# Block-sparse attention with a channel mix: wide units for the two end blocks only, scores in row groups by key slot, 32x32 turns on VectorE

## The chip, the cores and the metric

One core of one Trainium2 chip. The metric is the device time of one execution in microseconds; the median of three runs of the kernel before is 604.21 us (603.62 to 605.64).

## The reference

Two stages follow each other. The first is attention over 4 batches, 8 heads, 768 positions of 64 numbers, in blocks of 32 positions (24 blocks). A query block sees block 0, block 23, itself, its two neighbours and three blocks drawn at random; query blocks 0 and 23 see all. The second is a channel mix over the 512 joined channels.

```python
scores = scale * np.matmul(q, k.transpose(0, 1, 3, 2))
mask = np.abs(blk_i - blk_j) <= window                      # window = 1
mask = mask | (blk_i == 0) | (blk_j == 0) | (blk_i == n_blocks - 1) | (blk_j == n_blocks - 1)
for qb in range(n_blocks):
    for kb in sampled_blocks[qb]:                           # three, drawn; can repeat or be seen already
        mask[qb * block:(qb + 1) * block, kb * block:(kb + 1) * block] = True
scores = np.where(mask, scores, -1000000000.0)
attn = softmax(scores)                                      # rows' maximum subtracted, sum + 1e-09
x = attn @ v                                                # to (4, 768, 512)

xk = mu_k * x + (1.0 - mu_k) * x_prev                       # x_prev: x one position earlier
xr = mu_r * x + (1.0 - mu_r) * x_prev
k = np.maximum(xk @ w_k, 0.0)                               # 512 -> 1024
v = k * k @ w_v                                             # 1024 -> 512
r = 1.0 / (1.0 + np.exp(-(xr @ w_r)))
out = r * v
```

The three weights come as 64-bit floats and are narrowed on the chip.

## The kernel before

**Units.** Attention is cut into 24 units. Per batch there is one wide unit (u = 0) with the four query blocks 21, 22, 23 and 0 on 128 partitions, which takes scores against all 768 keys, and five near units (u = 1 to 5) with four consecutive query blocks each, 1 to 20. A query block of a near unit has eight slots of 32 keys: its neighbourhood (3), blocks 0 and 23, the three drawn. `load_unit` (L415) brings them by DMAs from SP's queue into one of five tiles KR per query block (the drawn ones at addresses read from `packed`), and the values into one of six tiles VR: the neighbourhood by a DMA on SP, block 23 and the drawn ones by an indirect gather on GpSimd (L470).

**A near unit** works in two groups (`near_group`), each of four heads. Scores `s` (L524): for each pair of heads, query block and head a product of 64 x 32 weights (the queries) with 256 key columns; two row halves and four column strips of the array work side by side. `soft` (L479, VectorE) scales, adds a mask per slot (a slot drawn twice, or seen already, gets a large number) and takes the row minimum in one pass, 256 columns at a time; `exp` (L489, ScalarE) follows with a sum of each row; `turn` (L500) turns 128 x 128 pieces on TensorE (PE) into `t`, copied to `pt` by VectorE (L506); the values `o` (L546) are products with 128 x 32 weights from `pt` and 64 columns of VR. `finish` divides by the sums, turns x (L606) and copies it into `xt`.

**A wide unit** (`wide_pair`) does the same for each pair of heads with 768 keys: `sw` (L563), `tw` (L500), `o` (L585).

**The mixer** handles each of 12 tiles of 256 positions: `split_x` forms xr and xk and splits them into two parts of lower precision, `gate` (L713, r), `hidden` (L731, h, then relu, square and its split), `values` (L760, v) with three products per term, and a last multiplication on VectorE (L768) and store (L771). `weight` narrows the weights at the start.

**Order.** Every operation is handed to `Plan.add` with its engine, a duration in ns, a rank, and what it reads and writes. `Plan.order` places all of them by these durations and ranks, and each engine's program is written out in that order; nothing is decided on the chip. The constants at the end of the file (O_MAX, LEAD_K and so on) set ranks and the earliest time that a load is placed. In the order before, the wide units of batches 0, 1 and 2 come first, those of batches 2 and 3 are kept in DRAM (`away`) and read back; the mixer's tiles have ranks at equal distances.

Sixteen KB of PSUM per partition are shared by s (two tiles of two banks), t (2), o (1) and m (1, the mixer's products).

Of the kernel before, what the change touches and what calls it, by code (L numbers as in the profile page):

```python
# [8 lines left out]
F32 = mybir.dt.float32  # L9
F32R = mybir.dt.float32r  # L10
I32 = mybir.dt.int32
# [5 lines left out]
DRAM = bass.MemoryType.DRAM  # L17

P = 128
# [10 lines left out]
QB, NC, SLOTS = 4, 5, 8  # L30

WIDE_BLOCKS = (NB - 3, NB - 2, NB - 1, 0)
SEEN = 5
FAR = 8e9

# [43 lines left out]
class Op:  # L79
    __slots__ = ("engine", "ns", "lag", "fn", "rank", "deps", "users", "bufs", "end", "start", "table", "seq", "waits", "release", "size")  # L80


class Plan:
# [13 lines left out]
    def add(self, engine, ns, rank, fn, reads=(), writes=(), lag=0, table=None, release=0.0, size=0):  # L97
# [5 lines left out]
        op.bufs, op.release, op.size = [], release * 1000, size  # L103
# [29 lines left out]

    def order(self):
        free, table, avail = {}, {}, {}
        queue_free = 0.0
# [6 lines left out]
        while len(placed) < len(self.ops):  # L143
            best = None
            for engine, ops in avail.items():
                now = free.get(engine, 0.0)
                cand = []
                for op in ops:
                    at = max(now, op.release)
                    for d in op.deps:  # L150
                        at = max(at, d.end + (self.HOP[d.engine] if d.engine != engine else self.SAME.get(engine, 60)) + d.lag)
# [7 lines left out]
                    if at is not None:  # L159
                        cand.append((at, op))  # L160
                if cand:
                    first = min(c[0] for c in cand)
                    now_on = table.get(engine)
                    at, op = min((c for c in cand if c[0] <= first + NEAR),
                                 key=lambda c: (c[1].rank - STAY * (c[1].table is not None and c[1].table == now_on), c[1].seq))
                    if best is None or at < best[0]:
                        best = (at, op)
            assert best is not None, "no operation can start"
            at, op = best
# [6 lines left out]
            op.start, op.end = at, at + ns  # L176
            free[op.engine] = op.end
            if op.size:
                ready = op.end + (self.RING_POOL if op.engine == "POOL" else self.RING)
                queue_free = max(queue_free, ready) + op.size / self.RATE  # L180
                op.lag = queue_free + self.DONE - op.end
            for buf in op.bufs:
# [22 lines left out]
AWAY = 2  # L205


def unit_time(i):

    wides = sum(u == 0 for b, u in UNITS[:i])  # L210
    others = min(i, len(UNITS)) - wides
    return A_FIRST + A_WIDE * wides + A_SOON * min(others, SOON) + A_STEP * max(others - SOON, 0)
# [3 lines left out]
def block_sparse_attention_channel_mix(  # L216
    ctx: ExitStack, tc: tile.TileContext,
    kt, kd, kq, qt, vt, vw, blocks, rows, picks, consts, mu_k, mu_r, w_k, w_v, w_r, out, wide,
# [5 lines left out]
    dr = ctx.enter_context(tc.tile_pool(name="scratch", bufs=1, space=DRAM))  # L224
# [14 lines left out]
    k_ring = buf([P, K_RING, S], F32, "k2", 1, "k_ring")  # L239
# [3 lines left out]
    number = fixed([1, NB * NRAND * 2], I32, "number")  # L243

    packed = fixed([1, NB], I32, "packed")
    lines = fixed([P, B, NC * QB], I32, "lines")
    near_mask = fixed([P, NC, SLOTS], F32, "near_mask")
    wide_mask = fixed([P, NB], F32, "wide_mask")
    mk = fixed([P, 2, CC], F32, "mk")
    early_w = buf([P, EARLY_W, 512, 2], I32, "wv", 1, "early_w")  # L250
    away = [Fixed(dr.tile([P, CC, P], F32, name=f"away{b}")) for b in range(B - AWAY)]


    def mask_setup():
        own = buf([P, NC + 1, NRAND, 2], I32, "kk", 3, "own")
        con = buf([P, NC * (SEEN + SLOTS) + 2 * NB + 2], F32, "zr", 3, "con")
        pick = buf([P, NC * QB, 2], I32, "kk", 3, "pick")
        f = buf([P, NC + 1, NRAND], F32, "dif", 2, "ownf")
        same = buf([P, NB * NRAND], F32, "x0", 1, "same")
        word = buf([P, 2 * NB], F32, "x1", 1, "word")  # L260
        line = buf([P, NC * QB], F32, "pt", PT_BUFS, "line")
        near = NC * SEEN
        stat = near + NC * SLOTS
        plan.add(SP, ISSUE, -30, lambda: nc.sync.dma_start(number.ap, blocks), writes=[(number,)], size=2000)
        plan.add(ACT, ISSUE, -32, lambda: nc.scalar.dma_start(own.ap.rearrange("p a b c -> p (a b c)"), rows), writes=[(own,)], size=20000)
        plan.add(ACT, ISSUE, -31, lambda: nc.scalar.dma_start(con.ap, consts), writes=[(con,)], size=60000)
        plan.add(ACT, ISSUE, PICK, lambda: nc.scalar.dma_start(pick.ap.rearrange("p a b -> p (a b)"), picks), writes=[(pick,)], size=20000)
# [11 lines left out]

        def find():  # L280
            v = nc.gpsimd
            c = con.ap
            v.tensor_copy(out=line.ap, in_=pick.ap[:, :, 0])
            v.tensor_scalar(out=line.ap, in0=line.ap, scalar1=c[:, stat + 2 * NB : stat + 2 * NB + 1],
                            scalar2=c[:, stat + 2 * NB + 1 : stat + 2 * NB + 2], op0=ALU.mult, op1=ALU.add)
            for b in range(B):
                v.tensor_scalar(out=lines.ap[:, b, :], in0=line.ap, scalar1=float(b * S), scalar2=None, op0=ALU.add)

        plan.add(DVE, 600, -15, pack, reads=[(number,)], writes=[(word,), (packed,)])
        plan.add(POOL, 900, PICK + 3, find, reads=[(con,), (pick,)], writes=[(line,), (lines,)])  # L290

        def far():
            v = nc.vector
            v.tensor_copy(out=f.ap, in_=own.ap[:, :, :, 0])
            c = con.ap

            e = same.ap.rearrange("p (a b) -> p a b", b=NRAND)
            v.tensor_tensor(
# [614 lines left out]
```

## Time and profile before

| | |
|---|---|
| median of three runs | 604.21 us |
| span of the profiled execution (its own time is not given beside it) | 616.1 us |
| TensorE busy (matmul) | 575.8 us, 93% |
| TensorE weight loads | 465.5 us, 76% |
| VectorE, ScalarE, GpSimd busy | 303.8, 300.6, 344.0 us |
| matmuls; instructions in all | 8172; 20666 |
| bytes moved by DMA | 114.18 MB, mean 185 GB/s |
| PE's share of the chain that ended last | 63% |

The span runs from the first to the last instruction. Rows of the profile give line, engine, operation, the names of what is written and read, shapes and count, then busy time and the mean of one, then the engine's idle time just before and what ended it; "issue" there is idle time that ended for nothing the profile shows. Rows of the timeline give start and length. Rows of stretches give for each engine busy time and count, then the granted clock of TensorE, the mean busy share of the 16 DMA engines, and GB/s.

### The profile page before, as it was taken

Reading aid. Unit: us, or ns where it says so; the run is one execution under the profiler, and the core shown is the slowest. Engines: PE = TensorE matmul, PEld = TensorE weight load, DVE = VectorE, ACT = ScalarE, POOL = GpSimd, SP = SyncE. Lnnn points to the kernel's source line nnn. Section 1 sums busy time; section 2 is a strip of 40 time slices with the busy share of each in tenths; the row PEclk is TensorE's granted clock in tenths of the full one; section 3 lists DMA queues with packets and bytes.
Section 4 is the critical chain, followed back from the end, with each engine's and each line's share of the span. In section 5 each row is a group of like instructions: output and inputs, shape, how many; then the busy total and the mean of one; then the engine's idle time right before and its main releaser. Section 6 shows DMA issues by size and latency. Waiting matters only on the chain.

```text
span 616.1 us, 20666 instructions
## 1 busy us (share of the span) xinstructions
PE 575.8 (93%) x8172; PEld 465.5 (76%) x8172; DVE 303.8 (49%) x906; ACT 300.6 (49%) x712; POOL 344.0 (56%) x400
## 2 busy tenths in 40 slices
PE   8887878798899999999999989999999999999997
PEld 3564655587667878878788778778778788989897
DVE  6677768873864255264443452653632532423300
ACT  3675845583544545355535534635545454333341
POOL 1324344865777737657836835546467464664551
PEclk9999989999899999999999999999999999999999
DMA  8959659858786667766764774774666620000001
GB/s 310 399 157 379 231 168 335 282 164 286 219 261 217 188 193 212 210 181 202 227 200 164 232 227 146 233 229 147 224 188 182 201 75 1 36 18 18 17 18 35
DMA packets 88499, 114.18 MB, mean 185 GB/s; under 512 B 12626, under 2 KB 59219, under 8 KB 88403
## 3 DMA queue, kind: packets, MB, share of 16 engines
q1 hardware_dynamic: 81570, 91.79, 46.7%
q0 software_dynamic: 6400, 20.98, 10.7%
q8 instruction: 65, 1.06, 0.7%
q10 hardware_dynamic: 432, 0.10, 0.2%
q14 instruction: 32, 0.25, 0.1%
HBM read 106.01 MB, written 6.82 MB: 183 GB/s over the span
## 4 chain that ended last, share of the span: by engine, by line
PE 63%; DVE 10%; ACT 8%; issue 6%; POOL 5%; DMA 3%; another core or an unknown queue 2%; SPq 2%; ACTq 0%; DVEq 0%; POOLq 0%
PE v L760 17%; PE o L546 5%; PE h_1p L731 5%; PE h_3p L731 5%; PE r_0p L713 5%; PE t L500 5%; PE r_1p L713 4%; PE h_2p L731 4%; ACT p L489 4%; PE s L524 3%; PE h_0p L731 2%; PE tw L500 2%; PE sw L563 2%; PE o L585 2%
## 5 line engine op out<-in xcount | busy, mean ns | idle before, releaser
L760 PE MATMUL v<-wv,k 128*128 128x512 f32 (+1 forms) x600 | 139.4, 386 | 1.4 <-DVE z L768 1.4
L760 PEld LDWEIGHTS v<-wv,k 128*128 128x128 f32 x600 | 107.5, 188 | 26.5 <-DVE xr_2f L680 2.1
L489 ACT ACTIVATE p<-p,nm 128x256 f32<-128x256 f32 x160 | 79.4, 498 | 48.7 <-DVE nm L479 48.7
L470 POOL DMA_INDIRECT VR<-vt,lines x80 | 79.0, 988 | 33.1 <-PE o L546 16.0
L506 DVE COPY pt<-t 128x512 f32<-128x512 f32 x80 | 53.0, 686 | 81.5 <-PE t L500 74.6
L479 DVE CUSTOM_DVE_ANT_1 p<-s,near_mask 128x256 f32<-128x256 f32 x160 | 57.9, 418 | 30.4 <-remote 19.4
L689 POOL TENSOR_TENSOR xr<-xr_1f,xr 128x256 fp32r<-128x256 f32 x24 | 17.7, 740 | 72.0 <-ACT xr L687 71.9
L524 PE MATMUL s<-KR,q 64*32 64x256 f32 x1280 | 50.8, 381 | 1.0 <-PE tw L500 0.9
L500 PE MATMUL t<-ident,p 128*128 128x128 f32 x320 | 47.5, 283 | 3.8 <-ACT p L489 2.3
L546 PEld LDWEIGHTS o<-VR,pt 128*32 128x32 f32 x2560 | 37.9, 110 | 15.0 <-issue 8.8
L546 PE MATMUL o<-VR,pt 128*32 128x64 f32 x2560 | 44.7, 221 | 2.3 <-issue 1.4
L687 ACT CAST xr<-xr_1f 128x256 fp32r<-128x256 f32 x24 | 9.7, 405 | 72.9 <-PE r_0p L713 43.0
L731 PE MATMUL h_1p<-xk,wk 128*128 128x256 f32 x288 | 37.0, 283 | 8.2 <-ACT h_0k L744 4.6
L609 DVE TENSOR_TENSOR x<-o,R 128x512 f32<-128x512 f32 x24 | 16.6, 691 | 56.8 <-PE o L546 53.7
L500 PEld LDWEIGHTS t<-ident,p 128*128 128x128 f32 x320 | 36.9, 144 | 9.3 <-ACT p L489 6.4
L731 PEld LDWEIGHTS h_1p<-xk,wk 128*128 128x128 f32 x288 | 34.7, 188 | 10.3 <-ACT h_0k L744 5.5
L731 PEld LDWEIGHTS h_0p<-xk,wk 128*128 128x128 f32 x288 | 34.9, 188 | 3.6 <-issue 3.3
L713 PE MATMUL r_1p<-wr,xr 128*128 128x512 f32 x144 | 37.7, 411 | 0.0
L524 PEld LDWEIGHTS s<-KR,q 64*32 64x32 f32 x1280 | 27.1, 105 | 13.8 <-issue 3.8
L731 PE MATMUL h_3p<-xk,wk 128*128 128x256 f32 x288 | 36.8, 282 | 0.4 <-ACT h_2k L744 0.4
L731 PEld LDWEIGHTS h_2p<-xk,wk 128*128 128x128 f32 x288 | 34.6, 188 | 3.3 <-ACT k L745 3.3
L731 PE MATMUL h_0p<-xk,wk 128*128 128x256 f32 x288 | 36.9, 283 | 0.0
(115 smaller groups left out, 1043.7 us busy)
## 6 DMA issues: line engine op xcount, KB each, us to landing
VR<-vw SPq DMA_DIRECT2D x80, 256.0 KB
KR<-kd SPq DMA_DIRECT2D x80, 192.0 KB
KR<-kt SPq DMA_DIRECT2D x240, 64.0 KB
k_ring<-kq SPq DMA_DIRECT2D x16, 384.0 KB
VR<-vt SPq DMA_DIRECT2D x24, 256.0 KB
q<-qt SPq DMA_DIRECT2D x23, 256.0 KB
out<-z SPq DMA_DIRECT2D x23, 256.0 KB
early_w<-w_k SPq DMA_DIRECT2D x8, 512.0 KB
```

The lines of the kernel that those rows point to most:

```text
L470: plan.add(POOL, GATHER, at - LEAD_V + 0.01 * j, lambda w=w, n=n: nc.gpsimd.indirect_dma_start(VR[w].ap[:, 1, :], None, vt.rearrange("b n ...
L479: nc.vector.tensor_tensor_reduce(out=p.ap[:, cs].rearrange("p (a x) -> p a x", x=BLK), in0=view().rearrange("p (a x) -> p a x", x=BLK), in ...
L489: plan.add(ACT, 280 + 0.83 * (cs.stop - cs.start), rank, lambda: nc.scalar.activation(p.ap[:, cs], p.ap[:, cs], AF.Exp, bias=nm.ap[:, col ...
L500: nc.tensor.transpose(tp.ap[:, i, :], p.ap[:, cs], ident.ap)
L506: plan.add(DVE, 600, rank + 0.1, lambda: nc.vector.tensor_copy(out=pt.ap, in_=tp.ap), reads=[(tp,)], writes=[(pt,)])
L524: nc.tensor.matmul(s.ap[ROWS[j], row, a * 256 : (a + 1) * 256].rearrange("p (n x) -> p n x", x=BLK), q.ap[half, hp, ROWS[j]], KR[keys[j]]. ...
L546: nc.tensor.matmul(o.ap[ROWS[j], h * D : (h + 1) * D], pts[i // 2].ap[:, 2 * (i % 2) + g, ROWS[j]], VR[values[j]].ap[:, g, h * D : (h + 1) ...
L609: plan.add(DVE, 600, rank, lambda: nc.vector.tensor_tensor(out=x.ap.rearrange("p (h d) -> p h d", d=D), in0=o.ap.rearrange("p (h d) -> p h ...
L689: plan.add(POOL, 80 + 2.4 * MIX * tw, rank + O_MIX, lambda f=f, cs=cs: nc.gpsimd.tensor_tensor(out=dst.ap[:, 1, cs], in0=f.ap, in1=dst.ap[ ...
L713: nc.tensor.matmul(pr.ap[:, 0:512], xr.ap[:, a, c, :], wr.ap[:, w, c, :], start=(c == 0 and m == 0), stop=(c == CC - 1 and m == 2))
L731: nc.tensor.matmul(ph.ap[:, ff * TT : (ff + 1) * TT], wk.ap[:, w, c, f * P : (f + 1) * P], xk.ap[:, a, c, :], start=(c == 0 and m == 0), s ...
L760: nc.tensor.matmul(pv.ap[:, 0:width], k2.ap[:, a, f, i * P : (i + 1) * P], wv.ap[:, w, f, cs], start=(f == 0 and m == 0), stop=(f == FC - ...
```

## The change

- Units: seven per batch. The wide unit now holds only query blocks 0 and 23; two heads stand side by side on the 128 partitions. Six near units hold blocks 1 to 22 in fours and threes (`GROUPS`). Each batch's wide unit is among the batch's first three; `away` goes.
- Near scores: partitions are now four groups of 32 rows, one for each pair of key slots, and the query blocks lie along the columns; a product has 64 columns (two slots). A row's maximum over all slots is then spread over four partition groups: VectorE takes maxima per group (`peak`), `spread` multiplies with slices of the identity on PE, VectorE takes the maximum over groups (`top`).
- `weigh`: VectorE scales and subtracts a whole group (1024 columns) in one pass, ScalarE takes exp in one pass without sums, and VectorE turns 32 x 32 squares; PE's turns and their copies go. The first two near units (`first_unit`) keep PE's turns.
- A slot that is drawn twice or seen already: its values are gathered from 32 rows of zeros at the end of `vt`. Each head's values have a 65th column of ones, so that the sum comes out of the value product; the masks and `soft` go.
- Keys: one of two KR tiles per unit, with the neighbourhoods of a unit in one load.
- PSUM: s 2 (two banks each), o 2, m 2; turns and spreads use m.
- The plan: it models PE's code in pieces of 257 instructions (`code`, `feed`) and eight loads in flight; durations are changed; each unit, mixer tile and weight has a rank of its own (`UNIT_AT`, `MIX_AT`, `WEIGHT_AT`, `RAW_AT`).

```diff
-QB, NC, SLOTS = 4, 5, 8
-WIDE_BLOCKS = (NB - 3, NB - 2, NB - 1, 0)
+QB = 4
+GROUPS = [(0, NB - 1), range(1, 5), range(5, 8), range(8, 12), range(12, 16), range(16, 20), range(20, 23)]
...
-    KR = [fixed([P, SLOTS, HP * BLK], F32, f"KR{i}") for i in range(KR_BUFS)]
-    VR = [fixed([P, 2, DM], F32, f"VR{i}") for i in range(VR_BUFS)]
+    KR = [fixed([P, KEYS * HP * BLK], F32, f"KR{i}") for i in range(KR_BUFS)]
+    VR = [fixed([P, 2, HD], F32, f"VR{i}") for i in range(VR_BUFS)]
...
-UNITS = [(0, 0), (1, 0), (2, 0), (0, 1), (0, 2), (3, 0)]
-UNITS += [(b, u) for b in range(B) for u in range(1, NC + 1) if (b, u) not in UNITS]
+UNITS = [(b, u) for b in range(B) for u in ((0, 1, 2) if not b else (1, 2, 0)) + (3, 4, 5, 6)]
...
+    CHUNK, FIRST, FETCHED, FLIGHT = 257, 204, 4600, 8
+    def feed(self, op, at, ns):
+        end, left, since = at, op.code, self.crossed
+        upto = self.upto
+        while left >= upto:
+            end += ns * upto / op.code
+            end = since = max(end, since + self.FETCHED)
+            left -= upto
+            upto = self.CHUNK
+        return end + ns * left / max(op.code, 1), since, upto - left
...
+    def peak(s, tops, many, width, name, rank, ns):
+        plan.add(DVE, ns, rank, lambda: nc.vector.tensor_reduce(
+            out=tops().rearrange("p (r c) -> p r c", r=2), in_=s.ap[:, :, 0 : many * width].rearrange("p r (c x) -> p r c x", x=width),
+            axis=AX.X, op=ALU.max), reads=[(s,)], writes=[name])
...
+            for i in range(QB):
+                for j in range(QB):
+                    nc.tensor.matmul(G.ap[ROWS[j], i, :], ident.ap[:, ROWS[i]], tops.ap[:, 0:many], start=True, stop=True, skip_group_check=True)
...
+    def weigh(s, p, base, many, width, rank, ns, kind):
+        size = 2 * many * width
+        def run():
+            nc.vector.scalar_tensor_tensor(
+                out=p.ap[:, 0:size].rearrange("p (r c x) -> p r c x", r=2, x=width),
+                in0=s.ap[:, :, 0 : many * width].rearrange("p r (c x) -> p r c x", x=width), scalar=SCALE,
+                in1=base().unsqueeze(3).to_broadcast([P, 2, many, width]), op0=ALU.mult, op1=ALU.subtract)
+        plan.add(DVE, 60 + 1.14 * size, rank + O_SUB[kind], run, reads=[(s,), ns], writes=[(p,)])
+        plan.add(ACT, 210 + 0.835 * size, rank + O_EXP[kind], lambda: nc.scalar.activation(p.ap[:, 0:size], p.ap[:, 0:size], AF.Exp), ...)
+        plan.add(DVE, 60 + 1.15 * size, rank + O_TR[kind], lambda: nc.vector.transpose(p.ap[:, 0:size], p.ap[:, 0:size]), ...)
...
+                for a in range(2):
+                    hp = 2 * gi + a
+                    for j in range(many):
+                        for i in range(QB):
+                            lo = END if i == QB - 1 else j + i
+                            hi = DRAWN + NRAND * j + i - 1 if i else DRAWN - 1
+                            for row, half in enumerate(HALF):
+                                x = (a * many + j) * 2 * BLK
+                                nc.tensor.matmul(
+                                    s.ap[ROWS[i], row, x : x + 2 * BLK].rearrange("p (n x) -> p n x", x=BLK),
+                                    q.ap[half, (hp * many + j) * BLK : (hp * many + j + 1) * BLK],
+                                    K[half, lo : hi + 1 : hi - lo, hp * BLK : (hp + 1) * BLK],
+                                    start=True, stop=True, skip_group_check=True)
...
-KR_BUFS, VR_BUFS, P_BUFS, PT_BUFS, T_BUFS, M_BUFS = 5, 6, 4, 4, 2, 1
+KR_BUFS, VR_BUFS, P_BUFS, PT_BUFS, M_BUFS = 2, 6, 4, 3, 2
...
-M_FIRST, M_STEP, M_LAST = 84.0, 41.265, 446.907
+UNIT_AT = [-31.20, -8.27, 1.57, 34.75, 52.07, 79.14, 85.99, 94.35, ..., 449.51, 468.91, 518.00, 525.29]
+MIX_AT = [55.59, 84.97, 127.86, 166.63, 217.92, 261.03, 303.95, 329.75, 425.44, 466.61, 519.30, 594.89]
```

More of the change, by code (lines that the diff above doesn't have):

```diff
@@ L247, in block_sparse_attention_channel_mix @@
-    near_mask = fixed([P, NC, SLOTS], F32, "near_mask")
-    wide_mask = fixed([P, NB], F32, "wide_mask")
+    lines = fixed([P, B, NEARS], I32, "lines")
     mk = fixed([P, 2, CC], F32, "mk")
     early_w = buf([P, EARLY_W, 512, 2], I32, "wv", 1, "early_w")
-    away = [Fixed(dr.tile([P, CC, P], F32, name=f"away{b}")) for b in range(B - AWAY)]
     def mask_setup():
[L255 to L259, printed above, removed]
+        number = buf([1, NB * NRAND * 2], I32, "dif", 2, "number")
+        con = buf([P, NEARS * SEEN + 3], F32, "zr", 3, "con")
+        pick = buf([P, NEARS, NRAND, 2], I32, "kk", 3, "pick")
@@ L278, in pack @@
             v.tensor_copy(out=packed.ap, in_=w)
+        plan.add(DVE, 1080, -15, pack, reads=[(number,)], writes=[(word,), (packed,)])
         def find():
[L281 to L287, printed above, removed]
@@ L324, in mask_setup @@
-        plan.add(DVE, 1100, -30, far, reads=[(own,), (con,)], writes=[(f,), (same,), (wide_mask,)])
-        plan.add(DVE, 3400, TWICE, twice, reads=[(f,), (con,)], writes=[(same,), (near_mask,)])
+            v.tensor_copy(out=r.ap, in_=pick.ap[:, :, :, 0])
+            first = r.ap[:, :, 0:1]
+            same = e.ap[:, :, 0:SEEN]
+            twice, keep, line = (e.ap[:, :, SEEN + i : SEEN + i + 1] for i in range(3))
+            v.tensor_tensor(out=same, in0=first.to_broadcast([P, NEARS, SEEN]), in1=c[:, 0:stat].rearrange("p (a b) -> p a b", b=SEEN), op=ALU.is_equal)
@@ L466, in load_unit @@
+        for j in range(many):
+            n = n0 + j
             w = place(1)
@@ L639, in block_sparse_attention_channel_mix @@
-    held = {}
+            for i, (p, x) in enumerate(parts):
+                nc.tensor.transpose(tp.ap[:, i, 0:size], p.ap[0:size, x : x + P], ident.ap[0:size, 0:size])
+        plan.add(PE, 128 * many, rank, tr, reads=[(ident,), *[(p, x // P // 3 if wide_p(p) else x // 256) for p, x in parts]], writes=[(tp,)], code=2 * many)
+        plan.add(ACT, 200 + 0.75 * size * many, rank + 0.1, lambda: nc.scalar.copy(pt.ap[:, 0:many, 0:size], tp.ap[:, 0:many, 0:size]), reads=[(tp,)], writes=[(pt,)])
+        return pt
@@ L660, in attention @@
-            finish(b, u, o, parts, L, t2 + O_END)
+                wide_unit(b, q, keys, values, o[0], t0, kind)
+                parts = [(i, row) for i in range(2) for row in range(2)]
+            else:
+                (first_unit if (b, u) in FIRST_UNITS else near_unit)(b, u, q, keys, values, o, t0, kind)
+                parts = [0]
+            finish(b, u, o, parts, t0 + O_END[kind])
     def split_x(b, which, t0, tw, name, rank):
```

611 lines of the change are left out of this document (323 added, 288 removed).

## The prediction

> **What bounds the kernel now.** I read the page first, then stretches, then the instructions of TensorE by line.
>
> ```profile
> span 616.1 us, 20666 instructions
> PE 575.8 (93%) x8172; PEld 465.5 (76%) x8172; DVE 303.8 (49%) x906; ACT 300.6 (49%) x712; POOL 344.0 (56%) x400
> ...
> q8 instruction: 65, 1.06, 0.7%
> ```
>
> ```profile
> 0.00:200.00 200.00, 171.56 (x3263) 123.78 (x3264) 137.08 (x383) 112.84 (x263) 105.05 (x130) 0.98 0.79 262
> 200.00:616.00 416.00, 404.28 (x4911) 341.70 (x4910) 166.76 (x525) 187.76 (x449) 238.93 (x271) 1.00 0.48 148
> ```
>
> TensorE (PE) is the bound: 28.4 of its 40.3 us of idle time lie in the first 200 us, and after that it is busy 97% of the time. The other engines are near half. So work taken off PE comes off the end, unless something new makes PE wait. PE's work by line, all fifteen groups:
>
> ```profile
> L760 PE MATMUL v<-wv,k 128*128 128x512 f32 (+1 forms) x600 | 139.4, 386 | 1.4 <-DVE z L768 1.4
> L524 PE MATMUL s<-KR,q 64*32 64x256 f32 x1280 | 50.8, 381 | 1.0 <-PE tw L500 0.9
> L500 PE MATMUL t<-ident,p 128*128 128x128 f32 x320 | 47.5, 283 | 3.8 <-ACT p L489 2.3 <-DVE pt L506 0.9 <-issue 0.3
> L546 PE MATMUL o<-VR,pt 128*32 128x64 f32 x2560 | 44.7, 221 | 2.3 <-issue 1.4 <-DVE pt L506 0.8
> L713 PE MATMUL r_1p<-wr,xr 128*128 128x512 f32 x144 | 37.7, 411 | 0.0
> L731 PE MATMUL h_1p<-xk,wk 128*128 128x256 f32 x288 | 37.0, 283 | 8.2 <-ACT h_0k L744 4.6 <-ACT p L489 2.6 <-issue 1.0
> L731 PE MATMUL h_0p<-xk,wk 128*128 128x256 f32 x288 | 36.9, 283 | 0.0
> L731 PE MATMUL h_3p<-xk,wk 128*128 128x256 f32 x288 | 36.8, 282 | 0.4 <-ACT h_2k L744 0.4
> L731 PE MATMUL h_2p<-xk,wk 128*128 128x256 f32 x288 | 36.7, 282 | 0.0
> L713 PE MATMUL r_0p<-wr,xr 128*128 128x512 f32 x144 | 36.4, 401 | 0.0
> L500 PE MATMUL tw<-ident,pw 128*128 128x128 f32 x192 | 27.9, 281 | 4.3 <-ACT pw L489 2.5 <-issue 1.0 <-ACT ptw L504 0.5
> L563 PE MATMUL sw<-k_ring,q 64*128 64x384 f32 x128 | 27.4, 522 | 4.9 <-DVE nmw L479 3.5 <-PE sw L563 1.0 <-PE tx L606 0.3
> L585 PE MATMUL o<-VR,ptw 128*32 128x64 f32 x1536 | 26.3, 220 | 5.4 <-issue 5.4
> L606 PE MATMUL tx<-ident,x 128*128 128x128 f32 x96 | 14.7, 276 | 4.5 <-DVE x L609 4.5
> L336 PE MATMUL warm<-const-bfloat16-1.0 128*128 128x512 bf16 x20 | 7.3, 547 | 0.8 <-PEq L861 0.8
> ```
>
> They add up to 607.5 us, and PE's busy time is 575.8, because neighbours overlap; a sum of rows is worth 0.948 of itself. The twenty near units take 50.8 + 47.5 + 44.7 + 20/24 of 14.7 = 155.2 us, the four wide ones 27.4 + 27.9 + 26.3 + 2.5 = 84.1. The mixer's work stays as it is.
>
> **PE's work after.** Prices come from groups of two sizes in the timeline:
>
> ```profile
> 13.56 0.92 PE L563 MATMUL sw<-k_ring,q 64*128 64x384 f32 x4
> ...
> 18.34 1.56 PE L563 MATMUL sw<-k_ring,q 64*128 64x384 f32 x8
> ...
> 146.11 0.65 PE L546 MATMUL o<-VR,pt 128*32 128x64 f32 x32
> ...
> 197.63 1.09 PE L524 MATMUL s<-KR,q 64*32 64x256 f32 x32
> ...
> 201.68 1.10 PE L546 MATMUL o<-VR,pt 128*32 128x64 f32 x64
> ...
> 216.98 1.96 PE L524 MATMUL s<-KR,q 64*32 64x256 f32 x64
> ...
> 240.86 0.60 PE L500 MATMUL t<-ident,p 128*128 128x128 f32 x4
> ```
>
> A fp32 product is two records (L524: 640 products in the code, x1280), a transpose is one. A 64-column record of L546 costs (1.10 - 0.65)/32 = 14.1 ns and the group 0.20 us; a 256-column record of L524 27.2 ns and 0.22.
>
> Scores of a near group (four blocks): 128 records of 64 columns in place of 32 of 256: the same columns. By columns, 6.8 ns each, 1.09 us as before; that is the low end. The high end is L546's pace, 128 x 14.1 + 0.2 = 2.00. I take the low one: L546 keeps four tiles of the array at work, L524 and the new scores eight, and L524's price by column, with half the tiles, is 13.6 ns for 64 columns, so L546 too is paced by columns. With three blocks: 0.87 (high 1.55).
>
> Spread of the row maxima (new): 32 records of 32 columns, 0.43 to 0.65 (half of L546's price; its row of x32); I take 0.45. The turns on PE go. Values: same records, 1.10 a group, 0.88 with three blocks. Turn of x: 0.60. A unit of four blocks: 2 x 1.09 + 0.45 + 2 x 1.10 + 0.60 = 5.43 (before 155.2/20 = 7.76); of three: 4.55. The first two near units keep turns: 7.4 and 6.5. There are now 24 near units: 15 x 5.43 + 7 x 4.55 + 13.9 = 127.2 us (high: 15 x 2.04 + 7 x 1.58 more, 168.9).
>
> A wide unit now has two blocks, two heads side by side: scores 32 records in four groups of 0.92 = 3.7 if four tiles run at once (else 4 x 1.56 = 6.2), six groups of turns 3.6, values 192 x 14.1 ns + 0.8 = 3.5, turn of x 0.35: 11.2, four times 44.6 (high 54.6).
>
> PE: 127.2 + 44.6 - 155.2 - 84.1 = -67.5, times 0.948: **-64 us** (high end: -15), so PE is busy 512 us. The warm records and the idle 40.3 stay.
>
> **Code of PE (the cost).** A near unit of m blocks issues 64m records of scores, 32 of the spread, 32m of values and 4 turns: 420 for four blocks, 324 for three; 16 and 8 of them, 144 fewer in the first two, 9,168. With 4 x 250 wide, 2,040 of the mixer and 20 of warming that is some 12,230, and as many weight loads, against 8172 of each: 1.5 times. The page's queue of instructions shows 65 packets in 1.06 MB, 16 KB each, about one per 252 of PE's 16,344 instructions. That fetching can be late is seen here:
>
> ```profile
> 22.27 0.98 PE L585 MATMUL o<-VR,ptw 128*32 128x64 f32 x53 [0.56 <-issue]
> ...
> 28.57 0.72 PE L585 MATMUL o<-VR,ptw 128*32 128x64 f32 x34 [2.42 <-issue]
> ...
> 34.76 0.49 PE L585 MATMUL o<-VR,ptw 128*32 128x64 f32 x18 [1.77 <-issue]
> ```
>
> ```profile
> 22.27:28.57 6.30, 3.88 (x128) 2.91 (x129) 4.36 (x11) 2.89 (x7) 2.33 (x3) 1.00 1.03 402
> 28.57:34.76 6.19, 4.42 (x128) 3.28 (x128) 1.17 (x4) 4.00 (x8) 1.48 (x2) 1.00 0.90 309
> ...
> 74.66:78.24 3.58, 3.58 (x146) 2.67 (x130) 3.48 (x15) 2.63 (x6) 1.41 (x2) 1.00 0.26 101
> ...
> 200.00:500.00 300.00, 292.27 (x4075) 242.09 (x4074) 137.04 (x443) 146.87 (x372) 180.14 (x212) 1.00 0.65 198
> ```
>
> PE stops in the midst of a row of like products, for nothing that the profile shows, and between two stops lie 257 and then 256 instructions: one packet. With the DMA engines 90% busy or more a packet's worth takes 6.2 to 6.3 us, and at 26% 3.58 sufficed; a line between them gives an estimate of 5.1 at the 65% of the middle stage. There PE now uses 8,149 instructions in 300 us, 9.4 us for 256: ample. After, some 97 packets; bytes hardly change (near keys shrink, gathers grow). All but two belong to the stage with attention: 95 x 5.1 = 485 us, against PE's 512 less 28 of the last tile and 8 of warming: 476. Even on average, so it is the bursts that tell: a near unit's 840 instructions are 16.7 us of fetching on 5.4 us of PE, a mixer tile's 336 (1.3 packets) lie on some 28 us of PE. Bounds: 0, and 630 - 552 = 78 us if each packet took 6.25 (95 x 6.25 + 36 = 630). The dense stretch above lost (0.56 + 2.42 + 1.77)/3 = 1.58 us a packet; I take two thirds of that, 1.05, for each of the 28 units, since mixer work now lies beside most of them: **+30 us**.
>
> The Trainium skill, "Runtime: NRT & Kernel Launch", section "Instruction fetch mechanics", says that fetching is hidden, as the sequencer issues more slowly than the buffer fills; the three stops above speak against it. By it this term is 0 and the sum 541.
>
> **The other engines** are costed at nothing; PE's work is what hides them.
>
> ```profile
> L479 DVE CUSTOM_DVE_ANT_1 p<-s,near_mask 128x256 f32<-128x256 f32 x160 | 57.9, 418 | 30.4 <-remote 19.4 <-PE s L524 8.3 <-PE tx L606 2.7
> L506 DVE COPY pt<-t 128x512 f32<-128x512 f32 x80 | 53.0, 686 | 81.5 <-PE t L500 74.6 <-DMA away<-hold 5.8 <-PE o L546 0.9
> L479 DVE CUSTOM_DVE_ANT_1 pw<-sw,wide_mask,nmw 128x384 f32<-128x384 f32 x32 | 18.8, 614 | 3.9 <-PE sw L563 3.3
> L479 DVE CUSTOM_DVE_ANT_1 pw<-sw,wide_mask 128x384 f32<-128x384 f32 x32 | 16.8, 552 | 1.7 <-PE sw L563 1.4
> ```
>
> ```profile
> L489 ACT ACTIVATE p<-p,nm 128x256 f32<-128x256 f32 x160 | 79.4, 498 | 48.7 <-DVE nm L479 48.7
> L489 ACT ACTIVATE pw<-pw,nmw 128x768 f32<-128x768 f32 x32 | 30.0, 938 | 11.8 <-DVE nmw L479 11.6
> ```
>
> VectorE: (552 - 418)/128 = 1.05 ns an element and 0.15 us; a pass over a group (1024) is 1.22 us. A near unit makes six (maxima, subtraction, 32x32 turn) and some 0.5 us of small ones: 7.8 us, 6.2 with three blocks, 174 in all, and the wide units 16 maxima of 0.96: 190, for 57.9 + 53.0 + 18.8 + 16.8 = 146.5 that go. With the halved finish that is some 50 us more, 355 of 580. A unit's chain (two maxima, spread, subtraction, exp, turn) holds both score banks some 8 us. Where no mixer work covers it, PE waits for the two subtractions before it can write the next scores, 2.4 us a unit; the four or five units ahead of the first mixer tile make that some 10 us, which I leave in the 28.4 us of early idle time. ScalarE loses about 75 us (exp of 1024 at 0.86 ns an element, 1.16 us, for four of 498 ns; no sums read). GpSimd issues eight gathers more and computes no line numbers. On SP's queue the drawn keys are 264 loads for 240, and a unit's keys now wait for all the scores two units before instead of block by block; behind them wait the value loads and the stores, but a unit is some 20 us, so the load comes a unit early still. The store and reload of two wide blocks go; with them a wait of VectorE of 5.8 us (row of L506), early, under other idle time: nothing.
>
> **Sum.** 616.1 - 64 + 30 = 582 us of span. The profile gives no time beside its span, which is 1.020 of the median of the runs, 604.21; so 582/1.020 = 571.
>
> **Rivals.** (a) Code comes in time, PE alone counts: 552 of span, 541. For it: no such stop after 100 us before. Against: the budget above is even. Chance 0.14. (b) Slower: fetching becomes the bound, as in the stretch at 22 to 35 us, through all of the attention stage: 630 of span, 618; it decides from 6.1 us a packet (95 x 6.1 + 36 = 616). For it: the DMA engines are 79% busy in the first 200 us. Against: 65% in the middle. Chance 0.16. (c) Small matmuls are paced by their number, at L546's price: PE -15 only, which in turn hides code, some 10 us of it left: 611, 599. For it: nothing shows eight tiles at 64 columns. Chance 0.10. "TensorE: Matmul & The Clock Gate" of the Trainium skill, Part 1, gives a floor of about 25 ns from start to start however few the columns; the trace's 14.1 ns is under it, and by the rule the scores would add some 90 us more. The forecast holds 0.60, its own range 552 to 592.
>
> **Range and chances.** 540 to 608: (a) to (c), cut short of (b). What tells from no change is 0.3%. Faster: 0.60 + 0.14 + most of (c), 0.80; same 0.04; slower 0.16.
>
> **What would show it.** Right: about 97 packets on the instruction queue; PE busy 505 to 525; groups of 128 score records near 1.1 us; "issue" before matmuls of 20 to 45 us in all; VectorE near 355. Wrong: score groups of 2 us (c); idle PE with "issue" over 80 us (b); PE waiting for VectorE's subtraction or turn by more than 30 us.

## The result, and the profile after

The changed kernel takes 628.78 us (median of four runs, 627.03 to 632.71), the kernel before 603.91 beside it: a ratio of 1.041 (95% interval 1.038 to 1.045), slower, where 571 us was forecast. The profiled execution took 628.26 us for a span of 626.4. One thing is needed to read the traces: chips differ. The profile of before, with its span of 616.1 us, fits a chip on which that kernel takes some 619 us (there a second profile of it has a span of 616.6); on the chip of the timed runs it takes some 604. Each ratio below is taken within one chip.

From the page of the changed kernel, the lines that answer to those of before:

```profile
span 626.4 us, 28087 instructions
...
PE 555.8 (89%) x12227; PEld 457.1 (73%) x12228; DVE 368.8 (59%) x670; ACT 251.5 (40%) x414; POOL 353.8 (56%) x402
...
q8 instruction: 96, 1.57, 1.1%
```

Between these two pages PE's work fell by 20 us, not by 64, and its idle time is 70.6 us. Where that lies, stretch by stretch (busy time and count of each engine, then the granted clock, the DMA engines' share, GB/s); first the changed kernel:

```profile
0.00:50.00 50.00, 21.23 (x364) 12.40 (x366) 22.09 (x51) 13.58 (x25) 12.41 (x19) 0.93 0.79 270
50.00:100.00 50.00, 28.85 (x1147) 23.66 (x1132) 41.08 (x61) 18.90 (x39) 38.96 (x42) 0.74 0.77 247
100.00:150.00 50.00, 39.50 (x1008) 32.18 (x1003) 44.19 (x62) 18.78 (x29) 39.86 (x46) 0.99 0.73 219
...
0.00:150.00 150.00, 89.58 (x2495) 68.24 (x2497) 107.36 (x173) 51.25 (x93) 91.24 (x106) 0.89 0.76 245
...
150.00:626.00 476.00, 466.24 (x9733) 388.91 (x9731) 261.44 (x499) 200.22 (x321) 262.54 (x297) 1.00 0.51 159
```

Then the kernel before:

```profile
0.00:50.00 50.00, 43.24 (x844) 27.14 (x844) 35.22 (x113) 29.85 (x59) 14.35 (x26) 1.00 0.83 290
50.00:100.00 50.00, 39.71 (x876) 27.10 (x876) 34.34 (x104) 29.90 (x76) 20.33 (x23) 0.97 0.78 267
100.00:150.00 50.00, 42.97 (x958) 33.48 (x957) 37.20 (x94) 29.55 (x70) 32.81 (x36) 1.00 0.78 251
...
0.00:150.00 150.00, 125.92 (x2676) 87.72 (x2677) 106.75 (x309) 89.30 (x203) 67.49 (x85) 0.99 0.80 269
```

After 150 us the changed kernel's PE is as full as before (466.2 of 476 us). In the first 150 it does 89.6 us of work instead of 125.9, and at a lower granted clock: 60 of its 70.6 idle us lie there. What PE waited for in that stretch (us in total, times, longest):

```profile
PE sw L651 <- DMA q<-qt: 16.3, 1, 16.3
PE s L524 <- issue: 12.0, 5, 3.4
PE s L603 <- DMA KR<-kt: 5.2, 2, 3.2
PE s L603 <- issue: 4.8, 2, 4.5
```

The first queries (L651) come after 16.3 us, behind weights in SP's order; then drawn keys are late, and PE stops for nothing that the profile shows. No single wait makes up the 60 us, so the start was taken apart by runs. The other part, PE's rows of the changed kernel by line:

```profile
L845 PE MATMUL v<-wv,k 128*128 128x512 f32 (+1 forms) x600 | 149.3, 394 | 3.4 <-issue 1.3 <-DVE base L537 1.1 <-POOL k L833 0.9
L524 PE MATMUL s<-KR,q 64*32 64x64 f32 x5184 | 70.3, 231 | 16.4 <-issue 14.8 <-DVE p L489 1.3
L553 PE MATMUL o<-VR,p 128*32 128x65 f32 x2592 | 50.2, 223 | 1.7 <-DVE p L497 0.9 <-issue 0.7
...
L568 PE MATMUL tw<-ident,pw 128*128 128x128 f32 x96 | 16.6, 304 | 2.3 <-ACT pw L581 2.3
L651 PE MATMUL sw<-KR,q 64*64 64x384 f32 x128 | 15.5, 572 | 19.7 <-DMA q<-qt 16.3 <-ACT pw L581 3.5
L681 PE MATMUL o<-VR,ptw 128*32 128x65 f32 x768 | 14.9, 226 | 0.8 <-ACT ptw L571 0.8
L480 PE MATMUL G<-tops,ident 128*32 128x32 f32 (+1 forms) x704 | 10.7, 199 | 1.5 <-issue 0.9 <-DVE tops L470 0.5
```

The scores (L524) are the largest miss: 70.3 us. From the timeline, single groups in the steady stage (start, length):

```profile
237.12 0.96 PE L845 MATMUL v<-wv,k 128*128 128x512 f32 x3
238.02 1.11 PE L553 MATMUL o<-VR,p 128*32 128x65 f32 x64
...
241.70 3.76 PE L845 MATMUL v<-wv,k 128*128 128x512 f32 x15
245.39 1.97 PE L524 MATMUL s<-KR,q 64*32 64x64 f32 x128
250.70 1.49 PE L524 MATMUL s<-KR,q 64*32 64x64 f32 x128
...
280.88 2.01 PE L524 MATMUL s<-KR,q 64*32 64x64 f32 x128
286.50 1.48 PE L524 MATMUL s<-KR,q 64*32 64x64 f32 x128
```

A record is one matrix product as the trace has it. The value groups take the 1.10 us forecast; the score groups 1.48 to 2.01 instead of 1.09. Longer and shorter groups take turns here; why is not known.

### The profile page after: what moved, and what is told of

Same layout as the page of the kernel before. It is cut to its first block, busy times and chain, and to the rows that moved or that the text cites. A ratio compares the mean times of both kernels' runs of the same rounds, so it can differ in the third digit from the quotient of the medians.

```text
span 626.4 us, 28087 instructions
## 1 busy us (share of the span) xinstructions
PE 555.8 (89%) x12227; PEld 457.1 (73%) x12228; DVE 368.8 (59%) x670; ACT 251.5 (40%) x414; POOL 353.8 (56%) x402
## 4 chain that ended last, share of the span: by engine, by line
PE 75%; DVE 9%; issue 5%; DMA 5%; POOL 3%; ACT 2%; SPq 1%; ACTq 0%; DVEq 0%; POOLq 0%
PE v L845 21%; PE s L524 10%; PE o L553 6%; PE h_0p L816 6%; PE r_0p L798 6%; PE h_1p L816 6%; PE h_2p L816 5%; PE r_1p L798 4%; PE h_3p L816 4%; DMA early_w<-w_k 2%; DVE wmag L349 2%; PE tw L568 2%; PE sw L651 2%; PE o L681 2%; DVE wf L353 2%
## 5 line engine op out<-in xcount | busy, mean ns | idle before, releaser
L845 PE MATMUL v<-wv,k 128*128 128x512 f32 (+1 forms) x600 | 149.3, 394 | 3.4 <-issue 1.3
L524 PE MATMUL s<-KR,q 64*32 64x64 f32 x5184 | 70.3, 231 | 16.4 <-issue 14.8
L524 PEld LDWEIGHTS s<-KR,q 64*32 64x32 f32 x5184 | 58.8, 108 | 31.7 <-issue 24.6
L470 DVE TENSOR_REDUCE tops<-s 128x16 f32<-128x1024 f32 (+1 forms) x44 | 49.5, 1130 | 48.0 <-PE s L524 48.0
L495 ACT ACTIVATE p<-p 128x1024 f32<-128x1024 f32 (+1 forms) x44 | 43.0, 988 | 34.1 <-DVE p L489 33.5
L553 PE MATMUL o<-VR,p 128*32 128x65 f32 x2592 | 50.2, 223 | 1.7 <-DVE p L497 0.9
L553 PEld LDWEIGHTS o<-VR,p 128*32 128x32 f32 x2592 | 43.1, 110 | 10.1 <-issue 6.3
L497 DVE STREAM_TRANSPOSE p<-p 128x1024 f32<-128x1024 f32 (+1 forms) x44 | 49.5, 1142 | 1.5 <-ACT p L495 1.4
L489 DVE SCALAR_TENSOR_TENSOR p<-s,base 128x1024 f32<-128x1024 f32 (+1 forms) x44 | 48.5, 1133 | 0.7
L853 DVE SCALAR_TENSOR_TENSOR z<-v,z 128x512 f32<-128x512 f32 (+1 forms) x25 | 16.6, 664 | 39.2 <-PE v L845 25.7
L798 PE MATMUL r_0p<-wr,xr 128*128 128x512 f32 x144 | 37.4, 404 | 0.0
L816 PEld LDWEIGHTS h_3p<-xk,wk 128*128 128x128 f32 x288 | 34.5, 188 | 3.3 <-issue 2.5
```

What stands on the lines that cost most here:

```text
L470: plan.add(DVE, ns, rank, lambda: nc.vector.tensor_reduce(out=tops().rearrange("p (r c) -> p r c", r=2), in_=s.ap[:, :, 0 : many * width]. ...
L489: nc.vector.scalar_tensor_tensor(out=p.ap[:, 0:size].rearrange("p (r c x) -> p r c x", r=2, x=width), in0=s.ap[:, :, 0 : many * width].rea ...
L495: plan.add(ACT, 210 + 0.835 * size, rank + O_EXP[kind], lambda: nc.scalar.activation(p.ap[:, 0:size], p.ap[:, 0:size], AF.Exp), reads=[(p, ...
L497: plan.add(DVE, 60 + 1.15 * size, rank + O_TR[kind], lambda: nc.vector.transpose(p.ap[:, 0:size], p.ap[:, 0:size]), reads=[(p,)], writes=[ ...
L524: nc.tensor.matmul(s.ap[ROWS[i], row, x : x + 2 * BLK].rearrange("p (n x) -> p n x", x=BLK), q.ap[half, (hp * many + j) * BLK : (hp * many ...
L553: nc.tensor.matmul(o[gi].ap[ROWS[j], i * DV : (i + 1) * DV], p.ap[:, at : at + BLK], VR[values[j]].ap[:, g, h * DV : (h + 1) * DV], start= ...
```

## The experiments

All edits are to the changed kernel unless "before" is said. Four explanations of the start were set against each other: its order, with the queries late (S in the expectations, which spell out their rivals); VectorE's narrowing of the weights (D); a lack of PE work that needs neither drawn keys nor weights, since only one wide unit now stands at the start instead of three (F); and the bytes to be brought (T). The table gathers what they gave; busy is PE's busy time in the first 150 us of the profiled execution, idle that of its whole span. Busy time alone can mislead: the same eight score groups kept PE busy for 14.7 us in the changed kernel, at a clock of 0.89 over the first 150 us, and for 17.5 us in the run with queries and warming first, at 0.77. So some places below give the number of score groups done by 150 us instead.

| run | ratio to before (95%) | busy to 150 | PE in all | idle |
|---|---|---|---|---|
| before again | one look, 618.51 us | 127.4 | 578.3 | 38.3 |
| the change again | 1.038 (1.033 to 1.043) | 91.3 | 558.5 | 69.9 |
| queries and warming first | 1.071 (1.068 to 1.073) | 92.8 | 574.6 | 86.9 |
| queries first | 1.044 (1.038 to 1.050) | 93.9 | 562.0 | 67.7 |
| few records | 1.003 (1.001 to 1.005) | 91.5 | 545.1 | 76.2 |
| few records, queries and warming first | 1.003 (1.002 to 1.005) | 94.7 | 547.5 | 71.5 |
| light narrowing | 1.037 (1.032 to 1.042) | 97.3 | 560.0 | 65.7 |
| before, light narrowing | 0.994 (0.991 to 0.997) | 129.4 | 570.4 | 26.5 |
| second wide unit early | 1.078 (1.071 to 1.085) | 79.3 | 559.3 | 87.1 |
| before, one wide unit early | 1.070 (1.066 to 1.074) | 98.9 | 582.9 | 61.4 |
| three suspects away | 0.982 (0.979 to 0.985) | 102.6 | 535.4 | 56.7 |
| short weights | 1.026 (1.022 to 1.031) | 95.5 | 555.7 | 67.4 |
| before, short weights | 0.994 (0.992 to 0.997) | 128.3 | 572.0 | 28.4 |
| short weights, three suspects away | 0.968 (0.964 to 0.973) | 111.6 | 537.0 | 47.1 |

"Before again", "queries and warming first", "few records" and "few records, queries and warming first" were run on the chip where the kernel before takes 619 us, all others on chips where it takes 605 to 606. The changed kernel itself was not run on the slower chip. So where a ratio of the last three of these is set against the 1.038 to 1.041 of the change, it is assumed that the chip slows both kernels alike, and no run shows that.

**Both kernels again.**

> The kernel before, unchanged, profiled once more. The prediction divided its span by 1.02, because the profiled execution of before (616.1 us) stood 2% over its runs (604.21), while the changed kernel's profiled execution (span 626.4) stands with its runs (628.78). If the 2% belonged to that one execution: a span of 602 to 606 here, and the missing 12 us lie in idle time or in the clock of the first 150 us. If profiling costs this kernel 2%: a span near 616 again.

> The changed kernel, unchanged, on a chip where the kernel before takes 619 us instead of 604, so that the other runs have their own reference. If the chip slows both alike: 640 to 648, ratio 1.04. If what slows the kernel before there (616 to 619) doesn't touch the changed one: 627 to 632, ratio 1.015 to 1.02. The first 150 us should again hold 50 us or more of idle PE, the rest 15 at most.

Before gave a span of 616.6 us and 618.51 of its own time, so its 2% go with the chip and not with profiling. The second run was meant for that chip, but its kernel before took 605.23 us: it repeats the first result with 1.038, and leaves open what the change does on the slower chip. Its "issue" waits are 17.1 us, 12.0 of them in the first 150 us, where the first profile had 24.5 and 20.4; a wait of 3.4 us near 90 us that the first profile gives to "issue" stands in this one as one of 3.6 us for VectorE's subtraction (L489).

**Queries first.** The first queries lead SP's queue; in the first run the warming products are moved to the front too.

```diff
-    for op in plan.order():
+    lead = {("SP", -60): -2.0, ("PE", -20): -1.0}     # second run: ("SP", -60) alone
+    for op in sorted(plan.order(), key=lambda o: lead.get((o.engine, o.rank), o.start)):
         op.fn()
```

> Only the start is reordered: the first wide unit's queries are the first load of SP's queue instead of behind six loads of weights, and the warming matmuls are PE's first instructions; every other instruction keeps its place. Theory S (the start's order is what the change lost): PE's first scores at 7 to 9 us instead of 16.25, and 8 to 16 us off the whole, 613 to 621. Theory R (the number of PE's instructions, by their issue and by the fetching of code): the next units are held by code and by keys anyway, at most 3 us off, 626 to 629.

> Only the first wide unit's queries are moved to the front of SP's queue; the warming matmuls stay at their place between the wide unit and the first near unit (36 us). With both moved the kernel took 661 to 664, with a granted clock of 0.77 in the first 150 us. If the warming's place sets the clock of the first near units: this one is 15 us or more under that, at or up to 8 us below the changed kernel. If moving the queries itself did the harm: within 5 of 663.

The wait for the queries is gone, and nothing is gained. What PE waited for in the first 150 us with the queries alone moved:

```profile
PE sw L651 <- ACT pw L581: 12.0, 1, 12.0
PE sw L651 <- DMA KR<-kq: 7.2, 1, 7.2
PE s L524 <- issue: 6.2, 3, 3.3
```

The first wide unit starts sooner and then waits for ScalarE's exp and for its own keys. With the warming moved as well, PE's clock is 0.77 over the first 150 us instead of 0.89, and the kernel takes 7% more than before. The clock is not shown to be the reason. By 150 us eight score groups are done, as in the changed kernel; the loss lies behind, where this run on the slower chip has 29.7 us of idle time instead of 10.2, 18.6 of it "issue" in many short stops within score groups:

```profile
260.81 0.88 PE L524 MATMUL s<-KR,q 64*32 64x64 f32 x66
262.03 0.32 PE L524 MATMUL s<-KR,q 64*32 64x64 f32 x4 [0.34 <-issue]
262.77 0.32 PE L524 MATMUL s<-KR,q 64*32 64x64 f32 x4 [0.41 <-issue]
```

Whether chip or edit brings them is open. With few records, next, moving queries and warming changes nothing (621.11 us with and without), though the clock falls from 0.86 to 0.76. So taking the late queries away brings nothing by itself.

**Few records.** A near group's scores as 16 products of 256 columns, which takes other keys than it should, but as many columns.

```diff
-                            for row, half in enumerate(HALF):
-                                x = (a * many + j) * 2 * BLK
...
-                                    K[half, lo : hi + 1 : hi - lo, hp * BLK : (hp + 1) * BLK],
+                    for i in range(QB):
+                        for row, half in enumerate(HALF):
+                            x, n = a * many * 2 * BLK, 2 * many
...
+                                K[half, i : i + n, hp * BLK : (hp + 1) * BLK],
```

> The near units' scores are issued as 16 products of 256 columns a group instead of 64 of 64 columns (each partition group takes neighbouring key slots for one query block, so the attention weights are other numbers); the array streams as many columns as before, the plan's order stays. Score records fall from 5,184 to 1,296, the code's packets from 96 to about 66. Theory R: score time on PE from 70.3 us to about 47, idle PE with issue from 24.5 us to under 10, together 588 to 600. Theory S: the steady part gains by the scores (about 15 us after 150 us), but the first 150 us stay at 55 us or more of idle PE, 610 to 616. If neither the pace of issue nor code matters: 626 to 629.

> Both edits: queries and warming first, and score products of 256 columns (other attention weights, as in the run with few records). If start and records are separate losses their gains add; if both are the same waiting (units that come late anyway), the sum is less than the parts. Theory R with S: 575 to 592. R alone: as with few records, 588 to 600. S alone: 600 to 608.

Groups of the steady stage, from the timeline of the first of these runs:

```profile
241.39 1.09 PE L521 MATMUL s<-KR,q 64*32 64x256 f32 x32
245.82 1.09 PE L521 MATMUL s<-KR,q 64*32 64x256 f32 x32
255.40 0.88 PE L521 MATMUL s<-KR,q 64*32 64x192 f32 x32
```

The same columns in a quarter of the records take 1.09 and 0.88 us, where the forecast had 1.09 and 0.87. So what the scores cost beyond it is their number, of products and of the weight loads that go with each; the run does not part these two. After the first 150 us, 36 score groups take 36.9 us here and 55.6 in the changed kernel: 19 us. A run below on a faster chip agrees (34 groups in 34.6 us). By the ratios the kernel gains some 3.6% of the kernel before, 22 us, if both chips may be compared; put on 604 us the ratio lies between what R and S expected. Within the slower chip there is one pair that differs by the records alone, queries and warming first without and with few records: 663.11 and 621.11 us, 42 us apart, 27 of them PE's work. The start does not get further: eight score groups by 150 us in both kernels, and the "issue" waits (9.7 us in all, with 66 packets of code) are replaced by waits for DMAs, VectorE and ScalarE.

**Light narrowing.** The shift and the sign pass are left out, 33 us of VectorE in the changed kernel and 23 in the kernel before.

```diff
-            plan.add(DVE, 430, rank, shift, ...
-            plan.add(DVE, 690, rank, sign, ...
+            plan.add(DVE, 430, rank, lambda: None, ...
+            plan.add(DVE, 690, rank, lambda: None, ...
```

> Two of VectorE's three passes that narrow each weight are left out (shift and sign; the weights are then other numbers), some 28 us of VectorE, most of it in the first 150 us; nothing else moves. Theory D (VectorE bounds the start: it was busy 41 and 44 of 50 us at 50 to 150 us, a near unit needs more of it than of PE): 12 to 25 us less than the changed kernel as measured beside it. Theory R (code and issue bound the start): at most 5 less. Theory L (loads bound the start): at most 3 less.

> The same two passes left out of the kernel before (other weights, as there). There wide units with twice as much PE as VectorE work stand at the start, so theory D expects less than in the changed kernel: 3 to 10 us off. If both lose the same, VectorE's start isn't what tells the two kernels apart.

The change gains 0.1%, within its interval, the kernel before 0.6%. In the changed kernel PE is busy 6 us longer in the start, at a clock of 0.84, and nine score groups are done instead of eight, but the end hardly moves. So these 33 us of VectorE's work are not what holds the start alone. The run of before also gives its idle time on this chip: 26.5 us.

**How many wide units stand early.** In the changed kernel the second batch's wide unit is put second (with its entry of `UNIT_AT`; the plan may then give a blocked buffer its turn); in the kernel before, the wide units of batches 1 to 3 go behind the near units of batch 0.

```diff
-UNITS = [(b, u) for b in range(B) for u in ((0, 1, 2) if not b else (1, 2, 0)) + (3, 4, 5, 6)]
+UNITS = [(0, 0), (1, 0)] + [(b, u) for b in range(B) for u in ((0, 1, 2) if not b else (1, 2, 0)) + (3, 4, 5, 6) if u or b > 1]
```

```diff
-UNITS = [(0, 0), (1, 0), (2, 0), (0, 1), (0, 2), (3, 0)]
+UNITS = [(0, 0), (0, 1), (0, 2), (0, 3), (0, 4), (0, 5), (1, 0), (2, 0), (3, 0)]
```

> The changed kernel with the wide unit of the second batch put second in the list of units, ahead of the near units of the first batch; all the work is as it was. Theory F (filler: the start lacks PE work that needs neither drawn keys nor weights): PE is busy 105 to 112 us in the first 150 instead of 92, and the ratio to the kernel before falls from 1.038-1.041 to 1.015-1.030. Theory J (the start is held by things that only the changed kernel's near units bring: the late queries, the drawn keys behind the weights, code, VectorE): the wide unit only shifts them, PE is busy 90 to 97 us there, ratio 1.035-1.045.

> The kernel before with the wide units of batches 1, 2 and 3 behind the five near units of batch 0 instead of among the first six units, so that one wide unit stands at the start, as in the changed kernel; all the work is as it was. Theory F: PE is busy 95 to 112 us in the first 150 instead of 127 to 129, and the time is 1.03 to 1.06 of the kernel before. Theory J: the near units of the kernel before bring none of what holds the changed kernel, they fill the place of the wide units; PE is busy 120 us or more there, ratio 0.99 to 1.015.

The kernel before, with one wide unit early, is 7.0% slower, with all its work and its own near units. Its first 150 us, and what PE waited for there:

```profile
0.00:150.00 150.00, 98.89 (x1881) 67.15 (x1882) 96.62 (x270) 62.89 (x161) 67.62 (x88) 0.84 0.82 278
```

```profile
PE s L524 <- DMA q<-qt: 17.3, 3, 8.4
PE tx L606 <- DVE x L609: 15.2, 6, 8.3
```

Some 27 us of PE's work are gone from the start, in F's range, and the clock fell from 0.99 to 0.84; the ratio is above the 1.03 to 1.06 that F expected. So the early wide units filled the start in the order before, and the near units of that kernel, put in their place, did not. But the run changes the order too: 17.3 us of its waits are for queries that now stand late in SP's queue, and all constants of the plan were chosen for the old order. How much of the loss is missing work and how much a plan that no longer fits, it does not part. The other run was a miss for both theories: a second wide unit early made the changed kernel worse. Its waits:

```profile
PE sw L658 <- DMA q<-qt: 16.3, 1, 16.3
PE s L610 <- ACT p L588: 11.7, 1, 11.7
PE tw L575 <- ACT pw L588: 9.7, 4, 5.3
```

ScalarE's exps are late in 21.4 us of it. That a wide unit now takes both of the two KR tiles, where it had tiles of its own before, may be the reason too, and so may constants chosen for another order; neither was tried. Moving the units cost time in both directions, so F has one run for it and one against.

**Three suspects away, and the bytes.** First the queries' order (SP alone), the narrowing and the records together; then the first twelve weight transfers cut to one eighth, alone, in the kernel before, and on top of the three.

```diff
+            n = 64 if i < 3 * CC else 512
-            plan.add(SP, ISSUE, at, lambda: nc.sync.dma_start(raw.ap.rearrange("p a b -> p (a b)"), src.bitcast(I32)),
+            plan.add(SP, ISSUE, at, lambda: nc.sync.dma_start(
+                raw.ap[:, 0:n].rearrange("p a b -> p (a b)"), src.bitcast(I32)[:, 0 : 2 * n]),
```

> The changed kernel with three suspects of the start taken away at once, each of which alone only handed its wait to the next: the first queries issued first, the shift and the sign pass of the weights' narrowing left out on VectorE, and the near scores as 16 products of 256 columns a group (1,296 instead of 5,184, on the wrong keys). Theory J (these three together are the start's loss): PE is busy 118 us or more in the first 150, and the time is 0.94 to 0.965 of the kernel before. Theory F: with them away the start still has too little work for PE, busy 92 to 106 us there; ratio 0.98 to 1.002, that of the run with few records alone (1.003) less what the narrowing gave the kernel before alone (0.006) and a little.

> The changed kernel with the first twelve weight transfers cut to one eighth (64 of 512 columns, which the narrowing then reads eight times over; instructions and their sizes are kept): 5.5 MB of the 36.8 MB of its first 150 us fall away. Theory T (the start is paced by bytes: PE work there is what the transfers bring, 89.6 us for 36.8 MB, 2.44 us a MB): PE is busy 98 to 104 us in the first 150 instead of 90, ratio to the kernel before 1.015 to 1.025. Theory O (order and engines, not bytes): PE is busy at most 94 us there, ratio 1.03 to 1.045.

> The kernel before with the same twelve weight transfers cut to one eighth, as a control: 40.4 MB bring 125.9 us of PE work in its first 150 us, 3.12 us a MB. Theory T: 5.5 MB less make room for up to 17 us of PE work, of the 24 us that are idle there; PE busy 133 to 143 us, ratio 0.972 to 0.987. Theory O: ratio 0.99 to 1.003.

> The short weight transfers added to the run in which three suspects were away (queries first, no shift and sign pass, few records), whose first 150 us held 102.6 us of PE and whose ratio was 0.982. Theory T: PE is busy 112 to 118 us there, ratio 0.958 to 0.972. Theory O: 100 to 106 us, ratio 0.975 to 0.986.

The first 150 us of these four, in that order:

```profile
0.00:150.00 150.00, 102.64 (x2001) 74.73 (x2007) 89.87 (x155) 57.09 (x101) 97.36 (x117) 0.90 0.83 266
```

```profile
0.00:150.00 150.00, 95.53 (x2640) 72.78 (x2641) 113.30 (x183) 54.89 (x97) 96.00 (x112) 0.87 0.70 214
```

```profile
0.00:150.00 150.00, 128.25 (x2699) 92.36 (x2700) 110.31 (x316) 92.33 (x211) 69.53 (x87) 0.97 0.73 239
```

```profile
0.00:150.00 150.00, 111.61 (x2142) 80.26 (x2143) 95.46 (x162) 60.60 (x106) 102.49 (x122) 0.89 0.77 239
```

Three suspects away at once bring 11 to 13 us of PE's time into the start, in F's range and far from the 118 of J (all of the loss is theirs). Fewer bytes alone bring 4 to 6 us and 1.2 to 1.5% of the time, between what T and its rival expected; on top of the three they bring 9 more, near T's range, and in the kernel before 0.6%, its rival's. So bytes are one of the limits, more of one the more of the others are gone, and not the pace of the start. With all four away PE still does 14 to 18 us less there than in the kernel before and its variants. In score groups done by 150 us: eight in the changed kernel, nine with light narrowing or short weights, ten with three suspects away, twelve with all four.

## Why the prediction was wrong, step by step

**"PE counts"** stood: after the first 150 us PE is busy 98% of the time, and what was taken off its work there came off the end (three suspects away: 33.5 us less work in that stage, 34.3 us less time).

**PE's work, -64 us: the step that failed and that turned the sign. Between the two pages it measured -20.** With -20 in place of -64 the sum would have been 616.1 - 20 + 30 = 626 us of span, 614 after the division, so slower; the other 15 us of the miss are idle time, below. By rows it was -67.5, and the rows of after sum to some 593 us against 607.5: -15. The largest part is the scores priced by columns: 15 x 2.18 + 7 x 1.74 = 44.9 us forecast for the 22 units, 70.3 measured, of 81.7 at the high end that it had worked out. The reasoning for the low end, that the value products are paced by columns and that twice the tiles halve the price, fails: without the group's 0.2 us, 64 columns on eight tiles cost 10.0 to 14.1 ns a record, 14.1 on four, where 6.8 was taken. The longer groups stand at the high end, 2.00. Rival (c) had the mechanism and -15, and missed the start: it came to 599. The Trainium skill, "TensorE: Matmul & The Clock Gate", Part 1, has a floor of about 25 ns from start to start; the score groups, 11.6 to 15.7 ns a record when the whole group is divided by 128, are under it, so here too the measurement decides. The second part was not in the sum: "the mixer's work stays as it is", but v went from 139.4 to 149.3 us. The trace shows where: other work now cuts v into some 59 unbroken pieces, some 30 before. Pieces of 3 and 15 records (0.96 and 3.76 us) give 0.23 us a record and 0.26 a piece, so 29 more pieces make 7.5 of the 9.9 us, an estimate from these two pieces; before with one wide unit early has some 26 pieces and 138.1 us. Part of a piece's price is overlap with its neighbours. The first two near units took 7.1 + 5.7 + 5.8 = 18.6 us without the turn of x (scores, turns, values), of 13.9 forecast with it; the value rows 50.2, of 45.3. Spread (10.7 of 9.9) and wide units (16.6 + 15.5 + 14.9 = 47.0, of 43.2) were nearly right.

**Code, +30 us: a wrong place.** There are 96 packets, 97 were forecast, and PE's waits for "issue" are 24.5 us, in the range of 20 to 45, but 17.1 in the second profile. The prediction had laid them on all 28 units as bursts; 4.1 us lie after the first 150 us (5.1 in the second). That comes close to the Trainium skill, "Runtime: NRT & Kernel Launch", "Instruction fetch mechanics", by which fetching is hidden, in the steady stage; in the start 20.4 us of such stops remain (12.0 in the second profile), and with fewer packets they turned into other waits. So in the steady stage on this chip the term was nearly nothing (on the slower chip, with queries and warming first, 18.6 us of "issue" lie there); what it is worth in the start is not shown, as no run changed the packets and nothing else. The 5.1 us a packet was an upper estimate, too: the 3.58 us at 26% had sufficed, and could have been more than was needed. (b) said slower, but not for what happened.

**"The idle 40.3 stay": the second step that failed, hidden by luck.** Idle time is 70.6 us and equals 40.3 + 30 only by chance: the stops forecast for all units did not come, and the start lost as much. On the chip of the timed runs the kernel before has a span of 602.0 us; PE's work of 570.4 us (the lower of its two variants in the table) to 575.8 (its page) leaves 26 to 32 us of idle time. So the account there is 15 to 20 us less work and 39 to 44 more idle time, together the 25 us of the result. The prediction put the 10 us of four or five uncovered near units into the early idle time of 28.4 us, as though the start stayed full; it had read the change of `UNITS`, priced the wide units that go and asked only for their work, not for what they covered. That PE does 34 to 38 us less in the first 150 us than in the kernel before is measured. That this is so because the early wide units are gone, the work that PE had while drawn keys, code and weights came in, is the likeliest reading and not shown: the kernel before loses 27 us there without them, in a plan made for another order, and one wide unit more did not help the changed kernel. What holds the near units there has no single answer: late queries, part of VectorE's work, or bytes, taken away alone, move the total by -1.5 to +0.6% of the kernel before, and few records gave their 19 us in the steady stage; ScalarE's work was not taken away in any run.

**The other engines.** VectorE at 368.8 us (355 forecast) and PE's waits for it at 9.0 us in all (less than 30) were right in the steady stage. In the start VectorE works 85 of the 100 us from 50 to 150, and that was not asked.

**The time from the span.** The two figures came, as it seems, from two chips. A span lies 1.9 us under its own time (626.4 and 628.26; 616.6 and 618.51); the division by 1.020 stood for the chip, and as a ratio it did no harm.

## What to carry to other kernels

Many small matrix products are priced by the row of a group with as few columns, or else by a range that keeps both ends; columns alone gave 1.09 us for what took up to 2.01. Work at the start of a kernel that needs few inputs may be worth what it covers, besides its own time: before shrinking it, read the stretch in which it runs and ask what the engine will do there instead. When idle time has several causes close behind each other, taking one away only names the next; take several away at once, and move the suspected cover in the kernel that still has it, knowing that a plan made for one order may lose by any other. Compare runs within one chip: three of these runs have no partner on theirs.

## What was not expected of the hardware

Score records of 64 columns on eight tiles take 11.6 to 15.7 ns each, in unbroken groups of 128 (1.48 to 2.01 us), where 32 records of 256 columns take 1.09 us, 34 ns each. PE's granted clock was lower in starts with more waiting: over the first 150 us 0.99 with 126 us busy, 0.89 with 90 and 0.81 with 79 (second wide unit early), in the kernel before 0.84 once its wide units were moved. It is not busy time alone, as 94 us gave 0.85 with the queries first, 93 gave 0.77 with the warming moved to the front as well, and 97 gave 0.84 with light narrowing. What the lower clock costs is not shown: with few records 0.86 and 0.76 gave the same time, 621.11 us. And one and the same program took 604 us on one chip and 619 on another, at 38 to 40 us of idle time on the slower one against 26 to 28 in close variants on the other.
